# A drain of GpSimd added in layer one of the last expert of an attention and mixture-of-experts kernel

## The chip, the cores and the metric

One core of one Trainium2 chip runs the program. The metric is device time in microseconds (us); the kernel before took 592.55 us as the median of 3 runs (592.47 to 593.56). All times of the trace are counted from the start of the profiled span.

## The reference

The program computes pooled attention and feeds its result to a mixture of experts. All data is float32.

```python
def _attn_ref(q, k, v):                      # q, k, v: 8 x 8 x 576 x 64
    k_p = k.reshape(B, H, Sp, 8, D).mean(axis=3)
    v_p = v.reshape(B, H, Sp, 8, D).mean(axis=3)
    scores = scale * np.matmul(q, k_p.transpose(0, 1, 3, 2))
...
    return np.matmul(attn, v_p)              # attn: softmax of scores

def _moe_ref(x, w_gate, w1, w2):             # x: 4608 x 512, 8 experts, 1024 hidden
    logits = x @ w_gate
...
    for e in range(E):
        mask = assigned == e                 # 576 tokens each
        h = np.maximum(x[mask] @ w1[e], 0.0)
        out[mask] = h @ w2[e]
```

The tokens are given to the experts greedily, the largest logit first, each token once, until an expert has its 576.

## The kernel before, in words

**Stages.** The attention (about the first 120 us) writes the tokens' vectors x to a scratch tensor `xd` in memory. A search on VectorE finds which tokens each expert gets. Then `experts` (from L1468) goes through the experts one after the other. For each it gathers the 576 token rows from `xd`, splits x and the weights into a high and a low part (`xh`, `xl`, `w1h`, `w1l`, `w2h`, `w2l`, so that three matmuls in the rounded type stand for one in float32), computes layer one (`stage1`, L1320: 16 groups of 12 matmuls, 8 of 256 columns and 8 of 320) and layer two (`stage2`, L1362, with `products`, L1369: five tiles of tokens), and scatters the result rows to the output.

**What GpSimd does there.** In this part of the kernel GpSimd issues transfers and hardly anything else. `fetch` (L1242) gathers rows with an indirect DMA. `scatter` (L1353) first writes one element called `spacer` (L1355) and then issues an indirect DMA from the result tile `yt` (or `yh`) to the output (L1356). Before the changed place it has issued 76 such transfers: 35 scatters, 33 gathers to `xa`, 7 to `xg` and one small one (`wake`, L1413). After it come 5 scatters.

**Order of the work.** The program is written out by hand in the order in which each engine is to work: the loop at L1656 takes one matmul of layer one after another from the generator `stage1`, counts them in `n` (0 to 191) and puts the small work of other engines between them by a planned clock (`advance`, `later`). In the last expert (`more` is false) at n = 48 the routing is tested for a case that the fast path can't handle (`R.suspect`, L1067, which computes `flag`), and at n = 136 every engine loads `flag` into a register (L1672). The last tile of the expert before is added on VectorE and scattered (L1403, L1404) while the last expert's layer one has begun.

**The end.** After the second tile of layer two of the last expert comes a branch on `flag` (L1459): its long side recomputes everything one expert after the other and is not taken here; its other side only sets the semaphores to the counts that the long side would have reached. On GpSimd that is one instruction for the semaphores of its transfers, INC_SWDGE_SEM, behind waits for the transfers. Then follow the last tiles of layer two, four scatters, and the end of the program (L1775): SyncE waits for every transfer's semaphore, and all five engines meet at two barriers, each of which begins with a DRAIN on every engine. The program's start (L1766) has one such barrier too. Nothing else in the kernel before issues a drain.

Of the kernel before, what the change touches and what calls it, by code (L numbers as in the profile page):

```python
# [1420 lines left out]
def kernel(ctx, tc, q, k, v, wblk, moe_w1, moe_w2, out):  # L1421
# [27 lines left out]
    with ExitStack() as c2:  # L1449
        rows = cst.tile([128, 6], I32, name="lastrows")  # L1450

        def keep():
            nc.vector.tensor_copy(rows[:, :5], R.rows)
            nc.vector.tensor_copy(rows[:, 5:], R.halves)


        X, flag, ps = experts(c2, tc, g, R, xd, moe_w1, moe_w2, out, A.ident, cap, keep)
        fast, X.scatters, X.fixed = X.scatters, [], True
        with tc.If(flag > 0):  # L1459
            experts_one_by_one(X, R, ps)  # L1460
            keep()
        X.scatters += fast
        X.put(1, ps, rows, rows[:, 5:], 7)
        for _ in X.stage2(7, rows, rows[:, 5:], range(2, 5)):
            pass


def experts(ctx, tc, g, R, xd, w1, w2, out, ident, cap, keep):  # L1468
# [3 lines left out]
    nc = tc.nc  # L1472
# [34 lines left out]
    def flush(left=0):  # L1507
        nonlocal dve
        while len(waiting) > left:
            due, t, f = waiting.pop(0)  # L1510
            f()
            dve = max(dve, due) + t

    def step(e):

        nonlocal now, ready, dve
        p, crit, t, what = held.pop() if held else next(g, (None, 0.0, 0.0, None))
        if p is None:
            return False
        if what == "id":  # L1520

            if p > e or p and pieces[p - 1].l < 8:
                held.append((p, crit, t, what))
                return False
            X.load_1(R.eid, 0, 4 if p else 2)
            eids[p] = R.eid
        elif what == "row0":
            X.fetch(R.rows, 0, X.xg[:, 0])
            warm(3)
        elif what == "rows":  # L1530
            if p and turned[p - 1] < 5:
                held.append((p, crit, t, what))
                return False
            X.gather(R.rows, direct(p), at, 0 if p else 1)
            toks[p] = R.rows, R.halves
            turned[p] = 0
        since[p, what] = now

        now += 0.2
        start = max(dve, now + 0.3)  # L1540
        ready, dve = start + crit + 0.1, start + t
        return t > 0

    def advance(e, t):

        nonlocal now
        now += t
        move(now)
        while True:
            if waiting and waiting[0][0] <= now:  # L1550
                flush(len(waiting) - 1)
            elif ready > now or not step(e):
                break

    def due(e, what, t):
        return (e, what) in since and now >= since[e, what] + t

    class Pieces:
# [12 lines left out]
        def next(self, ahead=True):  # L1571
            nonlocal dve
            if self.h == self.l:
                self.up()
            if ahead:
                self.up()
            self.low(self.e, self.l)
            dve = max(dve, now, self.at[self.l]) + 0.7
            self.l += 1
# [6 lines left out]
    def turn(e, t, name="tp", bufs=2):  # L1586

        nonlocal now
        if t not in direct(e):
            now = max(now, since[e, "rows"] + X.joined(e, t))  # L1590
            move(now)
            flush(1)
            X.xt_joined(t, later)
        else:
            now = max(now, since[e, "rows"] + lands(e, t) - 0.5) + 0.45
            flush(1)
            X.xt(t, name, bufs, later)
        turned[e] = t + 1
        if (e, t) == (0, 1):
            later(1.3, 0.2, lambda: X.load_1(behind(0), 2, 4))  # L1600
        if (e, t) == (0, 4):
            later(1.0, 0.2, lambda: X.load_2(behind(1)))
# [4 lines left out]
    def turns(e, upto, t0):  # L1607

        nonlocal last
        t = turned.get(e, 5)  # L1610
        if t < upto and due(e, "rows", lands(e, t) if t in direct(e) else X.joined(e, t)) and now >= last + 1.4:
            last = now
            turn(e, t)
# [36 lines left out]
    for e in range(8):  # L1650
        more = e < 7
        if e:
            X.load_2(eids[e])
        w1 = pieces[e]
        w2 = Pieces(e, X.high2, X.low2)
        for n, dt in enumerate(X.stage1(later, not e, last=not more)):  # L1656
            k = n if e else n - 64
            if 0 <= k < 48 and n % 2:
                w1.by(4 + (k + 2) // 8)
            if (10 if e else 2) <= n < 96:  # L1660
                turns(e, 5, n)
            for t in range(turned[e], {84: 5}.get(n, 0) if e else {4: 2, 24: 3, 60: 5}.get(n, 0)):
                turn(e, t)
            if n >= 64 and n % 2:
                i = n if e else n - 12
                w2.by((i - 70) // 14 if i > 70 else 0)
            if not more and n == 48:
                assert next(g, None) is None
                flag = R.suspect()
                keep()  # L1670
            elif not more and n == 136:
                flag = nc.values_load(flag[0:1, 0:1], min_val=0, max_val=1)  # L1672
            advance(min(e + 1, 7), dt)
        while w2.l < 8:
            w2.next()
        w1 = pieces[e + 1] = Pieces(e + 1, X.high1, X.low1)
        for n, dt in enumerate(X.stage2(e, *toks[e], range(5 if more else 1), later=later)):
            advance(min(e + 1, 7), dt)
            if more and due(e + 1, "id", 9):
                w1.by((n - 60) // 12 if n > 60 else 0)  # L1680
            if more:
                turns(e + 1, 3, n)
        if more:
            while e + 1 not in toks:
                now = max(now, ready)
                step(e + 1)
            while w1.l < 4:
                w1.next()
            for t in range(turned[e + 1], 2):
                turn(e + 1, t)  # L1690
        flush(2)
# [87 lines left out]
```

## Time and profile before

| | |
|---|---|
| median of 3 runs | 592.55 us |
| the profiled execution | 592.48 us |
| its span in the trace | 590.5 us |
| around the span (start and end of the execution) | 2.0 us |
| TensorE busy | 571.6 us, 97% |
| VectorE, ScalarE, GpSimd busy | 398.7, 305.7, 202.3 us |
| last matmuls end, last scatter issued | 581.3 us, 582.0 us |
| granted clock of TensorE over the span | 0.988 of full speed |

A row of an engine's queue has the engine's name with a q behind it (POOLq is GpSimd's sequencer, SPq SyncE's, PEldq TensorE's): drains, semaphore waits, branches and register loads stand there, and are counted as busy on no engine. A duration of such a row is the time for which it held its queue. POOL is GpSimd, SP SyncE, ACT ScalarE, DVE VectorE, PE and PEld TensorE's matmuls and weight loads.

### The profile page before, as it was taken

To read this page: it belongs to the slowest core of one execution; us is meant where nothing else is said; L and a number is where in the kernel's file an instruction comes from. 1 tells how busy PE (TensorE), PEld (TensorE's weight loads), DVE (VectorE), ACT (ScalarE), POOL (GpSimd) and SP (SyncE) were. 2 spreads that over 40 slices of the span, in tenths; PEclk is the share of its full clock that TensorE was granted. 3 is DMA by queue.
4 is the path that set the end of the run, shared out by engine and by line. 5 is a ranking of instruction groups with operands and counts; after the bars stand their busy time and mean duration, and the time that the engine had idled before them with its cause. 6 is when DMAs were issued, how large, how long until landed. Compare 5 with 4: busy or idle time off the path is not lost.

```text
span 590.5 us, 11108 instructions
## 1 busy us (share of the span) xinstructions
PE 571.6 (97%) x4014; PEld 509.1 (86%) x4014; DVE 398.7 (68%) x1175; ACT 305.7 (52%) x633; POOL 202.3 (34%) x292
## 2 busy tenths in 40 slices
PE   7999999997999999999999999999999999999993
PEld 4999999994997789779978988997899899889972
DVE  8677887887996789778976876597487346416200
ACT  6444455453451475386764575385549527935210
POOL 4999999971100500331122221212121212210021
PEclk9999999996999999999999999999999999999998
DMA  8999982214531774448439238454824654350010
GB/s 349 420 423 422 422 321 78 85 72 145 159 119 59 235 196 144 108 115 303 109 93 311 80 85 233 148 108 98 296 79 82 209 184 96 80 201 11 2 58 28
DMA packets 64017, 99.84 MB, mean 169 GB/s; under 512 B 34752, under 2 KB 34768, under 8 KB 61392
## 3 DMA queue, kind: packets, MB, share of 16 engines
q1 hardware_dynamic: 52704, 70.66, 36.7%
q0 software_dynamic: 5920, 18.89, 9.9%
q10 hardware_dynamic: 5328, 9.48, 4.2%
q8 instruction: 34, 0.56, 0.4%
q14 instruction: 31, 0.25, 0.1%
HBM read 72.40 MB, written 18.87 MB: 155 GB/s over the span
## 4 chain that ended last, share of the span: by engine, by line
PE 79%; issue 7%; POOL 5%; DMA 3%; DVE 3%; ACT 1%; SPq 1%; POOLq 0%; another core or an unknown queue 0%; ACTq 0%; DVEq 0%
PE h L1340 32%; PE h L1376 26%; PE psa L274 6%; PE pss L229 4%; PE h L1381 4%; DMA rawk<-in_k_dram 2%; PE pse L261 1%; POOL t L178 1%; PE rt L755 1%; POOL tk L165 1%; DMA xg<-xd,rows 1%; PE rt L261 1%; DMA out_dram<-yt,rows 1%; PE tp L1313 1%; PE rt L210 1%
## 5 line engine op out<-in xcount | busy, mean ns | idle before, releaser
L1356 POOL DMA_INDIRECT out_dram<-yt,rows x36 | 38.0, 1057 | 192.2 <-ACT yt L1396 167.1
L1376 PE MATMUL h<-w2l,hh 128*128 128x512 f32 x256 | 101.1, 395 | 0.0
L1376 PE MATMUL h<-w2h,hh 128*128 128x512 f32 x256 | 100.7, 393 | 0.3 <-PEq L1459 0.3
L1376 PE MATMUL h<-w2h,hl 128*128 128x512 f32 x256 | 100.7, 393 | 0.0
L1345 ACT ACTIVATE hh<-h 128x256 fp32r<-128x256 f32 (+2 forms) x129 | 52.9, 410 | 83.8 <-PE h L1340 83.4
L1340 PE MATMUL h<-xh,w1h 128*128 128x256 f32 (+2 forms) x516 | 92.8, 298 | 0.2 <-ACT xh L1315 0.2
L1340 PE MATMUL h<-xh,w1l 128*128 128x256 f32 (+2 forms) x516 | 91.4, 297 | 1.0 <-DVE w1l L1293 1.0
L1340 PE MATMUL h<-xl,w1h 128*128 128x256 f32 (+2 forms) x516 | 92.2, 298 | 0.0
L1244 POOL DMA_INDIRECT xa<-xd,rows x33 | 33.7, 1021 | 137.5 <-ACT xg L1267 42.1
L1340 PEld LDWEIGHTS h<-xh,w1h 128*128 128x128 f32 x516 | 76.7, 189 | 1.2 <-ACT xh L1315 0.5
L1340 PEld LDWEIGHTS h<-xh,w1l 128*128 128x128 f32 x516 | 76.2, 190 | 1.2 <-DVE w1l L1293 1.2
L1340 PEld LDWEIGHTS h<-xl,w1h 128*128 128x128 f32 x516 | 76.6, 190 | 0.1
L1350 DVE SCALAR_TENSOR_TENSOR hl<-h,hh 128x256 fp32r<-128x256 f32 (+2 forms) x129 | 57.0, 449 | 22.0 <-ACT hl L1348 9.9
L1396 ACT ACTIVATE yt<-h 128x512 f32<-128x512 f32 x32 | 19.2, 599 | 92.0 <-PE h L1376 71.4
L274 PE MATMUL psa<-vblk,eT 128*128 128x146 f32 (+4 forms) x390 | 59.8, 302 | 0.1
L1376 PEld LDWEIGHTS h<-w2h,hh 128*128 128x128 f32 x256 | 48.2, 188 | 9.7 <-issue 0.7
L1376 PEld LDWEIGHTS h<-w2l,hh 128*128 128x128 f32 x256 | 48.2, 188 | 9.3
L1376 PEld LDWEIGHTS h<-w2h,hl 128*128 128x128 f32 x256 | 48.1, 188 | 9.2
L274 PEld LDWEIGHTS psa<-vblk,eT 128*128 128x128 f32 (+1 forms) x390 | 50.9, 180 | 2.1 <-issue 1.1
L1293 DVE TENSOR_TENSOR w1l<-raw,w1h 128x512 fp32r<-128x512 f32 x64 | 41.7, 689 | 15.5 <-ACT w1h L1289 15.5
L1302 DVE TENSOR_TENSOR w2l<-raw,w2h 128x512 fp32r<-128x512 f32 x64 | 43.3, 683 | 3.0 <-ACT w2h L1299 2.7
L229 PE MATMUL pss<-kblk,rawq 128*128 128x144 f32 (+1 forms) x320 | 43.7, 293 | 1.3 <-PE psa L201 0.9
(273 smaller groups left out, 968.0 us busy)
## 6 DMA issues: line engine op xcount, KB each, us to landing
raw<-in_moe_w_dram SPq DMA_DIRECT2D x64, 512.0 KB, 6.0
xd<-xt ACTq DMA_DIRECT2D x36, 256.0 KB, 4.2
rawv<-in_v_dram SPq DMA_DIRECT2D x7, 1280.0 KB, 11.6
rawk<-in_k_dram SPq DMA_DIRECT2D x7, 1152.0 KB, 13.9
rawq<-in_q_dram SPq DMA_DIRECT2D x6, 1152.0 KB, 12.1
rawq<-in_q_dram SPq DMA_DIRECT2D x2, 640.0 KB, 10.5
rawk<-in_k_dram SPq DMA_DIRECT2D x2, 576.0 KB, 5.1
rawq<-in_q_dram SPq DMA_DIRECT2D x2, 512.0 KB, 10.3
```

The lines of the kernel that those rows point to most:

```text
L229: nc.tensor.matmul(ps[cols, j // 2, 144 * (j % 2):144 * (j % 2) + 144], self.q_of(b, j, n, cols.stop - cols.start), self.kblk[b % 4][:, j] ...
L274: self.nc.tensor.matmul(o[h], self.eT[i][:, c, h], self.vblk[b % 4][:, self.BLOCKS[c]:self.BLOCKS[c + 1], :n], start=(c == cs[0]), stop=(c ...
L1244: self.nc.gpsimd.indirect_dma_start(out=to[:n], out_offset=None, in_=self.xd, in_offset=bass.IndirectOffsetOnAxis(ap=rows[:n, t:t + 1], ax ...
L1293: self.nc.vector.tensor_tensor(l, raw, h.bitcast(F32), op=OP.subtract)
L1302: self.nc.vector.tensor_tensor(self.w2l[:, i], self.raw2[e][:, i], self.w2h[:, i].bitcast(F32), op=OP.subtract)
L1340: nc.tensor.matmul(ps[:, :m], a[:, j, fs], b[:, j, o], start=(n == 0), stop=(n == 11))
L1345: nc.scalar.activation(hh[:, f, o], ps[:, :m], AF.Relu)
L1350: later(0.65, 0.4, lambda f=f, o=o, m=m, ps=ps: nc.vector.scalar_tensor_tensor(hl[:, f, o], ps[:, :m], 0.0, hh[:, f, o].bitcast(F32), op0= ...
L1356: st = nc.gpsimd.indirect_dma_start(out=rows, out_offset=bass.IndirectOffsetOnAxis(ap=idx, axis=0), in_=y, in_offset=None)
L1376: nc.tensor.matmul(ps, a[:, f, o], b[:, f], start=(f == 0 and k == 0), stop=(f == 7 and k == 2))
L1381: nc.tensor.matmul(ps, self.hl[:, f, 512:], b[:, f], start=(f == 0 and k == 0), stop=(f == 7 and k == 1))
L1396: self.nc.scalar.activation(y, ps, AF.Copy)
```

## The change

A drain of GpSimd is issued in the loop of layer one of the last expert, after matmul number 24 of its 192 has been written down and before the test of the routing at n = 48. It is one more instruction in GpSimd's queue, without operands; rows of that kind are called DRAIN in the trace.

```diff
@@ -1664,6 +1664,8 @@
             if n >= 64 and n % 2:
                 i = n if e else n - 12
                 w2.by((i - 70) // 14 if i > 70 else 0)
+            if not more and n == 24:
+                nc.gpsimd.drain()
             if not more and n == 48:
                 assert next(g, None) is None
                 flag = R.suspect()
```

## Rows read from the trace of the kernel before

**Rows 1.** The page: span, then busy tenths of TensorE in 40 slices

```profile
span 590.5 us, 11108 instructions
...
PE   7999999997999999999999999999999999999993
```

**Rows 2.** The chain that ended last, its last piece: start us, us, what

```profile
581.72 1.20 POOLq L1775
```

**Rows 3.** Line 1775, window 581 to 582: ns min/median/max, first and last start

```profile
L1775 SPq EVENT_SEMAPHORE  x2: 28/1508/2988, 581.3 to 581.4; - x2
L1775 PEldq DRAIN  x1: 2365/2365/2365, 578.9 to 578.9; - x1
L1775 POOLq DRAIN  x1: 7901/7901/7901, 581.7 to 581.7; - x1
```

**Rows 4.** Line 1775, window 584 to 585: SyncE's own drains

```profile
L1775 SPq DRAIN  x2: 7/10/13, 584.8 to 584.9; - x2
```

**Rows 5.** Waits of SyncE's queue, window 575 to 591: total us, times, longest

```profile
SPq L1775 <- PEq L1775: 5.5, 2, 4.9
```

**Rows 6.** Stretches of the end: us, busy of PE, PEld, DVE, ACT, POOL, clock, DMA

```profile
585.00:587.00 2.00, 0.00 (x0) 0.00 (x0) 0.00 (x0) 0.00 (x0) 0.00 (x0) 0.89 0.00 0
587.00:590.50 3.50, 0.00 (x0) 0.00 (x0) 0.00 (x0) 0.00 (x0) 0.00 (x0) 0.50 0.00 0
```

**Rows 7.** GpSimd's other drains: line 1766, then line 1775 after 589.8 and 590.1

```profile
L1766 POOLq DRAIN  x1: 181/181/181, 0.3 to 0.3; - x1
...
L1775 POOLq DRAIN  x1: 113/113/113, 589.9 to 589.9; - x1
...
L1775 POOLq DRAIN  x1: 46/46/46, 590.2 to 590.2; - x1
```

**Rows 8.** The setting of GpSimd's transfer semaphores: line 1766, line 1459

```profile
L1766 POOLq INC_SWDGE_SEM  x1: 31/31/31, 0.1 to 0.1; - x1
...
L1459 POOLq INC_SWDGE_SEM  x1: 1728/1728/1728, 565.9 to 565.9; - x1
```

**Rows 9.** GpSimd's transfers, all: name, queue, count, median us to landing

```profile
out_dram<-yt,rows POOLq DMA_INDIRECT x36, 3.4
xa<-xd,rows POOLq DMA_INDIRECT x33, 3.5
...
xg<-xd,rows POOLq DMA_INDIRECT x7, 4.2
out_dram<-yt,lastrows POOLq DMA_INDIRECT x3, 3.1
...
norow<-in_moe_w_dram,ti POOLq DMA_INDIRECT x1, 2.5
out_dram<-yh,lastrows POOLq DMA_INDIRECT x1, 2.4
```

**Rows 10.** Timeline of GpSimd, 526 to 583: start, us, [idle before <-what ended it]

```profile
531.09 1.10 POOL L1356 DMA_INDIRECT out_dram<-yt,rows  x1 [3.28 <-DVE yt L1403]
536.21 0.09 POOL L1355 MEMSET spacer<- 1x1 f32 x1 [4.02 <-DVE hl L1350]
561.71 0.97 POOL L1356 DMA_INDIRECT out_dram<-yt,rows  x1 [25.41 <-ACT yt L1396]
...
581.96 0.97 POOL L1356 DMA_INDIRECT out_dram<-yh,lastrows  x1 [2.29 <-ACT yh L1409]
```

**Rows 11.** Timeline: first matmuls of layer one, VectorE beside GpSimd's transfer at 531.09

```profile
529.25 0.64 PE L1340 MATMUL h<-xh,w1h 128*128 128x256 f32 x4
...
531.34 0.41 DVE L1350 SCALAR_TENSOR_TENSOR hl<-h,hh 128x256 fp32r<-128x256 f32 x1
531.67 0.41 DVE L1282 TENSOR_TENSOR xl<-xg,xh 128x256 fp32r<-128x256 f32 x1
532.74 0.42 DVE L1350 SCALAR_TENSOR_TENSOR hl<-h,hh 128x256 fp32r<-128x256 f32 x1 [0.67 <-ACT hh L1345]
```

**Rows 12.** TensorE's waits, window 500 to 591, all of them

```profile
PE h L1376 <- PEq L1459: 0.3, 1, 0.3
```

## The prediction, made before the result was known

> **What bounds the kernel now.** I read the page first. TensorE is busy in nine tenths or more of nearly every slice, and only the last slice is clearly empty [rows 1]. So for some 580 us TensorE sets the pace, and GpSimd, where the change lies, could matter in the middle only if TensorE waited for it. The waits of TensorE from 500 us on hold one item, 0.3 us at the branch, and that is TensorE's own queue [rows 12]. What is left is the end. The chain that ended last closes there not with TensorE but with a row of GpSimd's queue at line 1775 [rows 2]. The view of that line, cut into short windows, gives the row its length: a DRAIN of GpSimd that begins at 581.7 and holds its queue for 7.9 us, to 581.7 + 7.9 = 589.6 [rows 3]. The span ends at 590.5 [rows 1].
>
> Is the drain only waiting for the last scatter? That scatter is issued at 581.96 and takes GpSimd 0.97 us, to 582.9 [rows 10]; it lands 2.4 us after its issue [rows 9], at 584.4. SyncE confirms it: its wait for the last transfer begins at 581.4 and takes 2.99 us, to 584.4 [rows 3]. TensorE's drain ends at 578.9 + 2.4 = 581.3 [rows 3], and SyncE reaches the barrier with its own drain at 584.9 [rows 4]. From then on no engine does anything and no transfer moves [rows 6]; SyncE sits in the barrier for 4.9 us [rows 5] (the view names PEq, but TensorE had long been done; the only row that is still open is GpSimd's drain). **So the last 5.2 us of the drain, 584.4 to 589.6, come after the last transfer has landed, and 589.6 - 584.9 = 4.7 us of them hold up the end of the program.**
>
> What does it do in that time? GpSimd's drains with no new transfer ahead of them take 181, 113 and 46 ns [rows 7], the last two right behind the long one. So the long one is not the price of a drain as such. The list of GpSimd's transfers counts 36 + 33 + 7 + 3 + 1 + 1 = 81 [rows 9], and no drain stands among them. A second instruction that deals with these transfers shows the same: INC_SWDGE_SEM takes 31 ns at the start, with no transfer issued, and 1728 ns at the branch, behind 77 of them [rows 8], some 22 ns for each. My reading is that each transfer leaves an entry behind, that the first drain goes through all entries, and that a later drain finds only those issued since. As an estimate from these rows, an entry costs 5.2 / 81 = 64 ns if the walk begins at the landing, or (589.6 - 582.9) / 81 = 83 ns if it begins when the last issue ends.
>
> The Trainium skill speaks against this. "VectorE: DVE Perf Modes", section "The DRAIN you can't avoid", says that the drains at a program's start and end are constant, about 12 ns, on all five engines. That holds here for SyncE's two (7 and 13 ns, [rows 4]) and not for GpSimd's (7901 ns, [rows 3]). By the page there is nothing in a drain that could be moved, and the time would stay as it is.
>
> **The change, part by part.**
>
> *The new drain itself.* It is one instruction in GpSimd's queue. In the written order it follows the scatter issued at 531.09, which is put down 0.8 us of planned time after the last expert's layer one begins, while matmul 24 comes about 3 us after; the next thing in the queue is the load of the flag, ahead of the memset at 536.21 [rows 10]. The issue ends at 532.2, and the transfer lands about 3.4 us after its start, at 534.5 [rows 9, 10]. 76 entries lie behind the drain (81 less the five scatters that follow). It ends at 532.2 + 76 x 0.083 = 538.5 or at 534.5 + 76 x 0.064 = 539.4. Queued behind it on GpSimd are the register load, the memset and the scatter of 561.71, which waits for ScalarE's result and before which GpSimd sits idle for 25.4 us [rows 10]. Even the later end leaves some 21 us. Nobody else waits for GpSimd in this stretch. Cost on the path: 0. If that cover were gone the whole 7 us would fall on the branch's semaphores and the scatters behind it. If the drain were put ahead of the scatter instead, it would end at about 535, the scatter would start then, and six entries would stay instead of five: still 0.
>
> *The drain at the end.* Five entries are left: the scatters at 561.71 and 581.96 [rows 10] and the three of `lastrows` [rows 9]. Bounds for what it then does after the landing: at least nothing, since five entries can be dealt with before the last one lands; at most the same 5.2 us, if the length does not go by entries but is paid once by any drain with a transfer ahead of it. Nothing in the trace can make it negative, because the last landing at 584.4 stays where TensorE's end puts it. I take 5 x 64 to 83 ns = 0.3 to 0.4 us, since the row nearest to this question, INC_SWDGE_SEM, goes from 31 to 1728 ns with the transfers behind it [rows 8]. The drain then ends at 584.4 + 0.4 = 584.8. What is late next is SyncE, which comes to the barrier at 584.9 [rows 4]. So of the 4.9 us that SyncE waited only the barrier's own hand-over, about 0.2, stays: the gain is 4.7 us, and not the whole 5.2.
>
> *The branch.* INC_SWDGE_SEM at 565.9 falls from 1.73 to some 0.1 us, with one entry behind it instead of 77 [rows 8]. ScalarE's copy and the scatter behind it may start over a us earlier. Nothing comes of that: TensorE doesn't wait for them [rows 12], and the last scatter hangs on TensorE's last matmuls through ScalarE's yh [rows 10].
>
> *Sum.* 592.48 of the profiled execution - 4.7 = 587.8 us. The profiled execution lies 0.07 below the median of the runs shown (592.55), less than the runs differ among themselves.
>
> **The rivals.**
>
> *The price is fixed (no change).* One drain after any transfers pays 5 us, however many, and the end pays it again for its last scatter. For it: the only long drain in the trace is also the only one with transfers just ahead, so the count and the mere fact of them can't be told apart by the drains alone. Against: INC_SWDGE_SEM above, and the issues of GpSimd's transfers, 1.10 us at 531 and 0.97 at 582 [rows 10], show no such fixed work. Time: 592.5. The rule of the skill named above would end at the same number.
>
> *The new drain keeps VectorE out (a part of the gain is lost).* If the walk shuts VectorE out of memory from 532.2 to 539.4, the subtraction that begins at 532.74 [rows 11] ends at 539.8. It frees one of five result banks, which TensorE, at 1.4 us a group (the distance of the two L1350 rows) from 529.25 on [rows 11], wants for its seventh group at about 537.9. TensorE would wait 2 us: 587.8 + 2 = 589.8, up to 590.2 with what queues up behind. Against: during GpSimd's transfer issue at 531.09 to 532.2 VectorE's subtractions run at 0.41 us, as they do at 532.74 without it [rows 10, 11]. The Trainium skill, "SBUF — State Buffer", section "SBUF: two separate sides", has a rule of this kind: VectorE instructions with two operands in SBUF and GpSimd's instructions share a pair of ports that one of them holds alone. L1282 at 531.67 is such an instruction, and no delay of it shows here.
>
> *The drain becomes a fence for all engines (slower).* If the other engines were made to wait for its end, as at the barriers of the end, TensorE would stand from matmul 24, at about 532.1 (two groups of 1.4 us after 529.25, [rows 11]), to 539.4: 7.3 us lost and 4.7 gained, 592.5 + 2.6 = 595.1. It decides as soon as TensorE stands for more than 4.7 us. For it: every other drain in this trace belongs to such a meeting. Against: those meetings need a drain and a semaphore wait on each engine, and the diff adds one call on one engine.
>
> *It doesn't do what it says.* The place is reached once, since n passes 24 in the last expert; for a drain that waits without taking entries away the time is that of the first rival, 592.5. The short drains behind the long one speak against it [rows 7].
>
> **How the numbers follow.** The forecast, 587.8, gets 0.81: the idle end is plain in the rows, and only the question of count or fixed price is open. The fixed price or a drain that leaves entries gets 0.10, VectorE kept out 0.05, the fence 0.04. A measurement of this kernel can tell about 0.2%, 1.2 us, from no change. Faster by more: 0.81 + 0.05 = 0.86; the same: 0.10; slower: 0.04. The range goes from 587.3 (the last landing and the hand-over half a us better) to 590.2, which takes in the residual of up to half of the 5.2 us and the VectorE case; it holds 0.86.
>
> **What would show it.** Right: a DRAIN row of GpSimd near 532 of some 6 to 8 us, the one at line 1775 ending by 585, SyncE's wait in the barriers near 0.8 us in place of 5.5, INC_SWDGE_SEM under 0.3 us, TensorE's matmuls as before and a span near 585.8. Wrong: the last drain still ending about 5 us after the last landing (fixed price), a gap of TensorE between 533 and 541 (VectorE or fence), or the memset behind the new drain later than 560.

## The result and the profile after

The changed kernel took 587.98 us (median of 6 runs, 587.72 to 588.26), the kernel before beside it 592.78 us (6 runs, 592.47 to 593.56). The ratio is 0.9918 with a 95% interval of 0.9908 to 0.9928: about 4.8 us less, clear of the 0.2% that can be told apart. The forecast was 587.8 us, with a range of 587.3 to 590.2.

| | before | after |
|---|---|---|
| profiled execution, its span (us) | 592.48, 590.5 | 587.91, 585.9 |
| the new drain of GpSimd (us) | none | 7.6, ends 538.6 |
| drain of GpSimd at the end (us) | 7.9, ends 589.6 | 2.9, ends 584.75 |
| SyncE's waits in the barriers, sum (us) | 5.5 | 0.7 |
| INC_SWDGE_SEM at the branch (ns) | 1728 | 203 |

First the page of the changed kernel, its span and TensorE's busy tenths, to be held against [rows 1]:

```profile
span 585.9 us, 11109 instructions
...
PE   7999999998999999999999999999999999999996
```

There is one instruction more, and the last slice, which was three tenths full, is six tenths full: the empty end has shrunk. The new drain has a line of its own, 1668 (columns: ns min/median/max, first and last start):

```profile
L1668 POOLq DRAIN  x1: 7620/7620/7620, 531.0 to 531.0; - x1
```

Line 1777 of the changed kernel is line 1775 of the one before. In the window 580 to 582, the rows that answer to [rows 3], and then, from 584.8 to 585.1, the one that answers to [rows 4]:

```profile
L1777 SPq EVENT_SEMAPHORE  x2: 28/1508/2989, 581.5 to 581.5; - x2
L1777 PEldq DRAIN  x1: 2365/2365/2365, 579.1 to 579.1; - x1
...
L1777 POOLq DRAIN  x1: 2912/2912/2912, 581.8 to 581.8; - x1
...
L1777 SPq DRAIN  x2: 7/10/12, 585.0 to 585.0; - x2
```

TensorE's and SyncE's rows are those of before, 0.1 us later. The drain of GpSimd is the one that has changed: 7901 ns became 2912 ns. Its last piece in the chain shows the start to the hundredth:

```profile
581.84 1.21 POOLq L1777
```

So it ends at 581.84 + 2.91 = 584.75, ahead of SyncE, which arrives at 585.0. SyncE's waits, window 570 to 591, against [rows 5]:

```profile
SPq L1777 <- DMA out_dram<-yh,lastrows: 3.0, 1, 3.0
SPq L1777 <- PEq L1777: 0.7, 2, 0.6
```

It still waits 3.0 us for the last scatter, and in the two barriers together 0.7 us instead of 5.5. These rounded sums are 4.8 us apart; less the 0.1 us by which SyncE arrives later, that is the 4.6 us between the two spans up to rounding.

The branch, line 1459, against [rows 8], and GpSimd's timeline around the new drain, against [rows 10]:

```profile
L1459 POOLq INC_SWDGE_SEM  x1: 203/203/203, 566.1 to 566.1; - x1
```

```profile
531.20 1.11 POOL L1356 DMA_INDIRECT out_dram<-yt,rows  x1 [3.27 <-DVE yt L1403]
539.26 0.09 POOL L1355 MEMSET spacer<- 1x1 f32 x1 [6.94 <-DVE hl L1350]
561.83 0.97 POOL L1356 DMA_INDIRECT out_dram<-yt,rows  x1 [22.48 <-ACT yt L1396]
...
567.54 0.97 POOL L1356 DMA_INDIRECT out_dram<-yt,lastrows  x1 [1.04 <-ACT yt L1396]
```

The memset behind the drain is 3 us later than before, and GpSimd still sits idle for 22 us ahead of the scatter at 561.83. (The drain itself is no busy time of the engine, so the view shows it as idle time and names VectorE, the flag's writer, as what ended it; VectorE's flag was there at 535.7.) VectorE beside the walk, which runs from the issue's end at 532.31 to 538.59; the first row is to be held against [rows 11]:

```profile
532.86 0.42 DVE L1350 SCALAR_TENSOR_TENSOR hl<-h,hh 128x256 fp32r<-128x256 f32 x1 [0.67 <-ACT hh L1345]
...
537.98 0.69 DVE L1302 TENSOR_TENSOR w2l<-raw,w2h 128x512 fp32r<-128x512 f32 x1 [1.81 <-ACT w2h L1299]
```

The lengths are those of the kernel before (0.42 us at 532.74 and 0.69 us at 537.86 there), and each row starts 0.12 us later, as the issue ahead of the drain does (531.20 against 531.09). TensorE's waits from 500 us on are again the single 0.3 us of [rows 12]:

```profile
PE h L1376 <- PEq L1459: 0.3, 1, 0.3
```

### The profile page after: what moved, and what is told of

Same layout as the page of the kernel before. It is cut to its first block, busy times and chain, and to the rows that moved or that the text cites. A ratio compares the mean times of both kernels' runs of the same rounds, so it can differ in the third digit from the quotient of the medians.

```text
span 585.9 us, 11109 instructions
## 1 busy us (share of the span) xinstructions
PE 572.4 (98%) x4014; PEld 509.4 (87%) x4014; DVE 399.2 (68%) x1175; ACT 306.2 (52%) x633; POOL 202.6 (35%) x292
## 3 DMA queue, kind: packets, MB, share of 16 engines
q0 software_dynamic: 5920, 18.89, 10.2%
## 4 chain that ended last, share of the span: by engine, by line
PE 80%; issue 7%; POOL 5%; DMA 3%; DVE 3%; ACT 1%; SPq 0%; POOLq 0%; ACTq 0%; another core or an unknown queue 0%; DVEq 0%
PE h L1340 32%; PE h L1376 26%; PE psa L274 6%; PE pss L229 4%; PE h L1381 4%; DMA rawk<-in_k_dram 2%; PE pse L261 1%; POOL t L178 1%; PE rt L755 1%; DMA xg<-xd,rows 1%; POOL tk L165 1%; PE rt L261 1%; PE h L584 1%; DMA out_dram<-yt,rows 1%; PE tp L1313 1%
## 5 line engine op out<-in xcount | busy, mean ns | idle before, releaser
L1302 DVE TENSOR_TENSOR w2l<-raw,w2h 128x512 fp32r<-128x512 f32 x64 | 43.3, 683 | 3.0 <-ACT w2h L1299 2.7
```

The source lines that it names most:

```text
L1302: self.nc.vector.tensor_tensor(self.w2l[:, i], self.raw2[e][:, i], self.w2h[:, i].bitcast(F32), op=OP.subtract)
```

## The experiments

The profile after rules out a price that every drain pays: the one at the end has five transfers ahead of it and is short. It leaves three readings of the long one. **A:** it goes through every transfer issued since the last drain, so much for each. **B:** only the first drain behind any transfer is long, whatever the number. **C:** it goes by the amount of data or rows that the transfers moved.

### The drain earlier: 26 or 46 transfers ahead of it, 55 or 35 behind

```diff
-            if not more and n == 24:
+            if e == 2 and n == 24:       # the other run: e == 4
                 nc.gpsimd.drain()
```

> The one drain stands in layer one of expert 2 instead of expert 7, behind 26 transfers and ahead of 55. Theory A (a drain goes through the transfers issued since the last drain, 83 ns each, from the end of the last issue on): the drain in expert 2 takes 26 x 0.083 = 2.2 us after the issue ahead of it, the drain at the end 55 x 0.083 = 4.6 us after the last issue, 2.6 us behind SyncE; 588.0 + 2.6 = 590.6 us. Rival B (the first drain behind any transfers pays about 6.3 us once, however many there are): the drain in expert 2 takes 6.3 us and the time is 588.0 us. No effect at all: 592.8 us.

Measured: 590.15 us against 592.51; ratio to the kernel before 0.9961 (0.9947 to 0.9975).

> The one drain stands in layer one of expert 4, behind 46 transfers and ahead of 35. Theory A: it takes 46 x 0.083 = 3.8 us after the issue ahead of it; the drain at the end 35 x 0.083 = 2.9 us after the last issue, 0.9 us behind SyncE; 588.9 us, and INC_SWDGE_SEM about 0.8 us. Were the entries walked from the last landing on at 64 ns each, the end would be 1.8 us behind SyncE, 589.8 us. Rival B: 6.3 us in expert 4, 588.0 us.

Measured: 589.03 us against 592.51; ratio 0.9938 (0.9922 to 0.9955). The lines of the drains and of the branch, expert 2 first (the row x3 holds the end's three drains, and its largest is the long one):

```profile
L1668 POOLq DRAIN  x1: 6047/6047/6047, 266.9 to 266.9; - x1
...
L1777 POOLq DRAIN  x3: 52/113/5776, 582.0 to 588.3; - x3
...
L1459 POOLq INC_SWDGE_SEM  x1: 1208/1208/1208, 566.6 to 566.6; - x1
```

```profile
L1668 POOLq DRAIN  x1: 5170/5170/5170, 374.5 to 374.5; - x1
...
L1777 POOLq DRAIN  x3: 52/113/4146, 582.6 to 587.3; - x3
...
L1459 POOLq INC_SWDGE_SEM  x1: 808/808/808, 566.8 to 566.8; - x1
```

B is out: both kernels have a drain behind transfers early on, and both pay a long one again at the end, in the order of the transfers that are left. Against 7901 ns with 81 transfers, the end's drain is 2125 ns shorter with 26 fewer and 3755 ns shorter with 46 fewer: 81.7 and 81.6 ns for each. The end's drain comes 2.6 us and 1.0 us behind SyncE's arrival in the two traces (587.74 against 585.09, 586.73 against 585.73), where A said 2.6 and 0.9. The reading in which the walk begins only at the last landing (64 ns each) expected 1.8 us for expert 4 and is out. The times follow, 2.2 us and 1.1 us over the changed kernel.

One miss: the drain in expert 2 should have held its queue, after the issue ahead of it, for 26 x 0.083 = 2.2 us. That issue ends at 268.28 (its row is at 267.18 and takes 1.10 us), the drain at 266.94 + 6.05 = 272.99, which is 4.7 us later. The transfer was late here. All of its packets stand in the window 270.5 to 271.6 (queue, packets, MB, share of the DMA engines), and the trace has the last update of its semaphore at 271.88:

```profile
q0 software_dynamic: 48, 0.13, 29.7%
```

But that isn't the whole of it, for the drain ends another 1.1 us after the landing. The section on the drains side by side takes this up.

### The drain when everything has long landed

```diff
-            if not more and n == 24:
+            if not more and n == 150:
                 nc.gpsimd.drain()
```

> The drain stands at n = 150 of layer one of the last expert, behind the load of the flag, when the last transfer ahead of it has long landed. Theory A: the row of the drain holds nothing but the walk, 76 x 0.083 = 6.3 us from about 536.2; the time is that of the changed kernel, 588.0 us. If a part of the drain of the changed kernel was the wait for the landing, with 64 ns an entry behind it: 4.9 us, the time the same.

Measured: 588.09 us against 592.51; ratio 0.9927 (0.991 to 0.9943).

```profile
L1668 POOLq DRAIN  x1: 6271/6271/6271, 536.4 to 536.4; - x1
```

This row holds nothing but the walk: 6271 / 76 = 82.5 ns for each transfer. The time is that of the changed kernel within what can be told apart, so the place within the idle stretch doesn't matter. The changed kernel's own drain fits the same figure: its issue ends at 531.20 + 1.11 = 532.31, and 76 x 0.0825 = 6.27 later is 538.58, where it ended. So with 76 transfers the landing of the last one, in between, cost nothing on top.

This kernel also shows VectorE beside the walk better than the changed one. Four subtractions of L1302, which read two operands from SBUF, lie wholly inside the drain (536.4 to 542.7); the kernel before, in the same window 537 to 542, comes second:

```profile
L1302 DVE TENSOR_TENSOR w2l<-raw,w2h x4: 681/688/693, 538.1 to 541.0; 128x512 fp32r<-128x512 f32 x4
...
L1302 DVE TENSOR_TENSOR w2l<-raw,w2h x4: 685/690/692, 537.9 to 540.7; 128x512 fp32r<-128x512 f32 x4
```

The walk doesn't slow them.

### More transfers, hardly more data

Sixteen small gathers of 4 rows of 64 bytes are issued where the change has its drain, first without a drain and then with one behind them. Both kernels do this work beyond what the reference asks, and its result is not used.

```diff
+            if not more and n == 24:
+                tiny(nc, R, wk, w_2, 16)    # 16 x nc.gpsimd.indirect_dma_start, 4 x 16 floats each
+                nc.gpsimd.drain()           # in the second kernel alone
```

> The kernel before without a drain, and with 16 more gathers of 4 rows of 64 bytes each, at n = 24 of layer one of the last expert, where GpSimd is idle. They hold 0.07 MB of 18.9. Theory A (cost by the number of transfers): the drain at the end takes 16 x 0.083 = 1.3 us more, 9.2 us, and INC_SWDGE_SEM 16 x 0.02 = 0.3 us more, 2.05 us; 592.8 + 1.3 = 594.1 us. Rival C (cost by the rows or bytes that were moved): under 0.1 us more, 592.8 us. Rival B (fixed): 592.8 us.

Measured: 593.67 us against 592.72; ratio 1.0019 (1.0009 to 1.0029).

```profile
L1787 POOLq DRAIN  x3: 46/113/9207, 581.5 to 591.3; - x3
...
L1468 POOLq INC_SWDGE_SEM  x1: 2048/2048/2048, 565.7 to 565.7; - x1
```

The drain grew by 9207 - 7901 = 1306 ns, 81.6 ns for each of 16 transfers that moved 16 x 4 x 64 bytes, 4 KB together (the 0.07 MB of the expectation was too much): C is out. Nor does the price go by packets: the 16 gathers add 512 to the queue's 5920 (5920 are 73 for each of 81 transfers, 512 are 32 for each of 16), at the same price for each transfer. The time grew by 0.95 us, a little less than the 1.3 of the drain; its profiled execution came to the end 0.2 us earlier than that of the kernel before (581.5 against 581.7).

> The same 16 gathers with the drain behind them. Theory A: the drain goes through 92 transfers, 92 x 0.083 = 7.6 us behind the last gather's issue at about 553, to 560.6, just ahead of the scatter at 561.7; at the end five are left; 588.0 us as in the changed kernel. If the last gather is issued later than 554, the scatter of 561.7 moves, with no effect on the end. Rival C: 6.3 us for the drain, 588.0 us.

Measured: 587.67 us against 592.72; ratio 0.9917 (0.99 to 0.9933).

```profile
L1679 POOLq DRAIN  x1: 16265/16265/16265, 543.2 to 543.2; - x1
...
L1788 POOLq DRAIN  x3: 46/112/2912, 581.6 to 585.3; - x3
```

```profile
551.00 0.88 POOL L1424 DMA_INDIRECT tinyrow<-in_moe_w_dram,ti  x1 [0.30 <-issue]
560.12 0.09 POOL L1355 MEMSET spacer<- 1x1 f32 x1 [8.24 <-issue]
561.57 1.04 POOL L1356 DMA_INDIRECT out_dram<-yt,rows  x1 [1.37 <-ACT yt L1396]
```

Here the row of the drain misleads if it is read alone. It begins at 543.2, when GpSimd has seven gathers still to issue, and lasts 16.3 us; what counts is the time from the last issue's end, 551.88, to the row's end, 559.46: 7.58 us for 92 transfers, 82.4 ns each. It came in 2 us ahead of the scatter at 561.57, and the end's drain is the short one again.

### The drain where nothing hides it

```diff
             self.nc.scalar.activation(y, ps[:, :256], AF.Copy)
+            self.nc.gpsimd.drain()
             self.scatter(self.out.rearrange("n (a d) -> (n a) d", a=2), halves, y)
```

> The drain stands right ahead of the last scatter, where no other work hides it. Theory A: it starts at the end of the issue before, 579.7, goes through 80 transfers in 6.6 us, to 586.3; the last scatter is issued at 586.6 instead of 582.0, lands at 589.0, and the end comes at 590.3 of the span, 592.3 us, the same as before (592.8). Rival B: 6.3 us, 592.0 us. If a drain in the middle cost GpSimd nothing: 588.0 us.

Measured: 592.98 us against 592.51; ratio 1.0006 (0.9996 to 1.0015): no change.

```profile
L1410 POOLq DRAIN  x1: 7824/7824/7824, 578.9 to 578.9; - x1
...
L1776 POOLq DRAIN  x1: 2722/2722/2722, 587.4 to 587.4; - x1
```

```profile
579.13 0.97 POOL L1356 DMA_INDIRECT out_dram<-yt,lastrows  x1 [4.37 <-ACT yt L1396]
586.79 0.09 POOL L1355 MEMSET spacer<- 1x1 f32 x1 [6.69 <-issue]
587.57 0.97 POOL L1356 DMA_INDIRECT out_dram<-yh,lastrows  x1 [0.69 <-issue]
```

```profile
SPq L1776 <- DMA out_dram<-yh,lastrows: 8.1, 1, 8.1
SPq L1776 <- PEq L1776: 0.7, 2, 0.5
```

The wait has only moved. In the barriers SyncE waits 0.7 us, as in the changed kernel, but it waits 8.1 us in place of 3.0 for the last scatter, which stands behind the drain. So the gain comes from the cover, the idle 25 us of GpSimd, and not from a drain as such. The median is 0.7 us over what A expected. The profiled execution, at 593.27 us the longest of the ten, ends at 591.4 of the span where A said 590.3. About half of that is the whole end coming 0.5 us later than in the kernel before (the issue ahead of the drain is at 579.13 instead of 578.61), and about half the last issue, which came 0.69 us after the memset where 0.2 was allowed for. Why, the rows don't say.

### One more instruction that is no drain

```diff
             if not more and n == 24:
-                nc.gpsimd.drain()
+                nc.gpsimd.memset(X.spacer, 0.0)
```

> In place of the drain one more memset of the spacer: one more instruction of GpSimd at the same place. All theories that put the gain down to the drain: 592.8 us, the drain at the end 7.9 us. If any further instruction at this place did it (by moving the instructions behind it): 588.0 us.

Measured: 592.69 us against 592.72; ratio 0.9998 (0.9989 to 1.0008).

```profile
L1777 POOLq DRAIN  x3: 46/113/7902, 582.2 to 590.7; - x3
```

The same long drain (7902 against 7901 ns): that one more instruction stands there does nothing.

### The drains side by side

The part of a row ahead of the last issue's end is 1.2 us at the end of the program (the drain's start at 581.72 to 582.93, [rows 2, 10]).

| kernel, drain | transfers since the last drain | row, us | from the last issue's end, us | per transfer, ns |
|---|---|---|---|---|
| before, end | 81 | 7.90 | 6.70 | 83 |
| expert 2 alone, end | 55 | 5.78 | 4.57 | 83 |
| expert 4 alone, its own | 46 | 5.17 | 3.83 | 83 |
| expert 4 alone, end | 35 | 4.15 | 2.94 | 84 |
| 16 more gathers, end | 97 | 9.21 | 8.00 | 82 |
| 16 more gathers and the drain, its own | 92 | 16.27 | 7.58 | 82 |
| ahead of the last scatter | 80 | 7.82 | 6.62 | 83 |
| n = 150 | 76 | 6.27 | 6.27 (whole row; the last issue had long ended) | 82 |
| expert 2 alone, its own | 26 | 6.05 | 4.71, with the landing | |
| changed kernel, end | 5 | 2.91 | 1.70, with the landing | |

The walk does not run wholly beside the landing. Where the last transfer lands late against the walk, what the drain still takes after the landing grows with the transfers too:

| kernel, drain | transfers | landing, us | drain's end, us | after the landing, us |
|---|---|---|---|---|
| ahead of the last scatter, end | 1 | 590.02 | 590.08 | 0.06 |
| changed kernel, end | 5 | 584.52 | 584.75 | 0.24 |
| expert 2 alone, its own | 26 | 271.88 | 272.99 | 1.11 |
| expert 4 alone, end | 35 | 585.26 | 586.73 | 1.47 |

(The landing is the end of SyncE's wait for that scatter, and for expert 2 the last update of its semaphore.) That is some 42 ns for each, half of the 82. (Beside expert 2's drain other transfers were moving some 400 GB/s; at the other three ends nothing else moved, and they lie on the same line.) So the rows fit two goes through the list of about 41 ns a transfer each: one from the last issue's end, the other not before the last landing. With a long list the first go outlasts the landing and the sum is 82 ns for each from the issue's end; with a short one the end is the landing and 42 ns for each. With 41 ns for each go and 0.04 us on top, this account gives the end of all eleven drains of the two tables to 0.03 us. It was read from the rows afterwards, and no run was made to test it.

None of these kernels beats the changed one by more than can be told apart, and the rows say why none is to be had from the drain: it ends 0.2 us ahead of SyncE now. After the landing at 584.52 there are 0.46 us until SyncE arrives at 584.98, so by the second table some 10 transfers (an estimate: 0.46 / 0.042 = 11, and 0.24 us are taken by five), not more, could stand behind the last hidden drain before the end would feel it.

## Why the prediction was right

**The reading of the end.** That the 4.7 us in which SyncE sat in the barrier were GpSimd's, and not TensorE's as the view's row named it, was right: the wait went with the drain. Of the 4.7 the profiled executions show 592.48 - 587.91 = 4.57; the rest is TensorE's end, 0.12 us later in the execution after. The medians differ by 4.8, since the kernel before measured 592.78 over six runs, 0.23 more than over the three that the forecast started from.

**Entries, and their price.** That the long drain goes through the transfers one by one was argued from one pair of INC_SWDGE_SEM rows and is now shown, by number and not by data. Of the two prices offered, 64 and 83 ns, the second is right for every long list, counted from the last issue's end. Its account, a walk that simply runs beside the landing, is not quite right: a part that grows with the number, some 42 ns a transfer, comes after the landing.

**What stays at the end.** The forecast put 0.3 to 0.4 us for five entries behind the landing, 5 times 64 to 83 ns; measured are 0.24 us. The term was of the right kind and too large, since only about half of a transfer's price falls behind the landing. It had no effect on the sum, because SyncE is later still, as foreseen.

**The cover.** The new drain ended at 538.6, the earlier of the two ends given. The load of the flag moved from 535.6 to 538.6, the memset from 536.2 to 539.3, and 22 us of idle time were left where 21 were expected. That the cover is what pays is shown by the drain ahead of the last scatter.

**The branch.** INC_SWDGE_SEM fell to 203 ns (about 100 expected). The 31 ns at the program's start, from which the forecast took 22 ns a transfer, are not the foot of that line: the rows of all kernels lie on some 183 ns and 20 ns for each transfer. The scatter behind it went out at 567.54 instead of 568.80 and nothing followed from it, as forecast.

**The rivals.** The fixed price fell with the profile after, and its variant, a fixed price for the first drain, with the kernels of experts 2 and 4. No fence: TensorE's only wait is the one of before. VectorE was not kept out: beside the walk its subtractions take as long as before, 0.42 us, and with two operands in SBUF (L1302) 681 to 693 ns against 685 to 692. So nothing here shows the shared ports of the Trainium skill, "SBUF — State Buffer", at work in a drain; the page limits its rule for two-operand instructions to a GpSimd instruction that reads SBUF, and no run here shows whether a drain does. Nor do the 12 ns that the Trainium skill gives for the drains at a program's start and end ("VectorE: DVE Perf Modes", "The DRAIN you can't avoid") hold for GpSimd's: the first drain behind its transfers took 2.7 to 9.2 us at the end of these kernels. The page speaks of drains that the runtime adds, while these stand at a line of the kernel, so it may never have been about them.

## What to carry to other kernels

Look at the rows of the engines' queues behind the last matmul, not only at busy time: a drain of GpSimd that ends long after the last transfer has landed is work put off, in these kernels 82 ns for every transfer that GpSimd has issued since its last drain. One drain late in the program, where GpSimd is idle for longer than that sum and nothing urgent is queued behind it, takes this work off the end; put where nothing hides it, it gains nothing. Keep few transfers behind it. Fewer and larger transfers from GpSimd might save the same at its source, which was not tried.

## What the runs showed of the hardware that was not expected

The price of a transfer in a drain didn't depend on its kind: 16 gathers of 256 bytes cost 81.6 ns each, and the scatters and gathers of up to 256 KB that fill the rest of the list come to 82 to 84 ns. By the second table of the drains about half of that price is not paid before the last transfer has landed. INC_SWDGE_SEM goes by the same list at a quarter of the price: 203, 808, 1208, 1728 and 2048 ns with 1, 31, 51, 77 and 93 transfers since the last drain, 20 ns for each on top of some 183. And issuing a transfer doesn't get dearer as the list grows: 0.97 us with 80 behind it before, and 0.97 with 4 after the change.
